# Loading keys and queries twice instead of copying the rounded half across partitions

## The chip, the core and the metric

The kernel runs on one core of a Trainium2 chip. Five engines take part: TensorE (PE in the profile; PEld is its weight load), VectorE (DVE), ScalarE (ACT), GpSimd (POOL) and SyncE (SP), which here issues every DMA. The metric is the device time of one execution in microseconds (us). Before the change the median of three runs is 737.69 us (737.01 to 740.85).

## The reference

Three layers follow one another on B = 4 sequences of S = 576 positions. The first is attention with H = 8 heads of D = 64 and a bias from a running sum:

```python
scores = scale * np.matmul(q, k.transpose(0, 1, 3, 2))
cum = np.cumsum(np.maximum(s, 0.0), axis=-1)
bias = -(cum[:, :, :, None] - cum[:, :, None, :])
scores = np.where(causal, -1e9, scores + np.minimum(bias, 0.0))
attn = softmax(scores)            # max, exp, sum + 1e-9
x = matmul(attn, v)               # then heads side by side: [B, S, 512]
```

The second layer is a gated feed-forward block (w_in 512 x 1024, GELU, normalisation, a 576 x 576 mixing matrix w_sg, w_out), and the third a block with squared ReLU and a sigmoid gate (w_k, w_v, w_r). All products are in fp32 precision: each operand is split into a rounded part (fp32r, "hi") and the rest ("lo"), and hi*hi, hi*lo and lo*hi are summed.

## The kernel before, in words

The scores of a head are two matmuls with 128 contraction rows each (L236 and L237). For the first, `qa` holds the rounded query in partitions 0 to 63 and the query's rest in 64 to 127, and `ka` holds the rounded key in both halves: one matmul gives hi*hi + lo*hi. For the second, `QB` holds the rounded query in 64 to 127 and `KB` the key's rest there, and partitions 0 to 3 of both carry ones and the running sum (the bias), split in hi and lo.

A head's operands come about so. `kq` is loaded by one DMA of 128 partitions: keys in 0 to 63, queries in 64 to 127 (L202). A cast rounds the query into `QB[64:128]` (L214: on DVE, for head 0 on ACT), another rounds the key into `ka[0:64]` (L215: on DVE for heads 1 to 7, else on ACT). Since an engine's lanes don't cross partitions, two DMAs inside SBUF copy the rounded query to `qa[0:64]` (L216) and the rounded key to `ka[64:128]` (L217). GpSimd computes the two rests (`split_lo`, L66 with tiles `KB` and `qa`). Two small DMAs bring the running sum into `QB` and `KB` (L207, L208), from the tile `crt` for the first sequence and from `cumd` in DRAM later.

`kq`, `qa` and `ka` have two buffers each; `QB` and `KB` have two fixed tiles, and a third borrowed set (names ending in `_f`) for the first sequence. Heads are worked on in pairs (`attn_pair`): score chunks of up to 512 columns go into two PSUM buffers `sc`; DVE adds the mask and takes the row minimum of the negated scores (L261), ACT takes the exponential (L269), PE transposes the result (L284, L287, L295), and the products with V follow (L317). In the first sequence a `prologue` converts the weights w_in and w_sg between the score steps: for w_in ACT L73, DVE L74, L75 and L77, ACT L80, POOL L66 (tiles `syt`, `wv`). From the second sequence on the attention of the next sequence is interleaved with the feed-forward matmuls (L346) of the one before. The third layer follows attention.

The order on each engine is not written out by hand: a scheduler sets it when the program is built, from its own timeline. Every engine, SP with its DMA issues too, executes its list in that order, and a row that waits holds back those behind it.

Of the kernel before, what the change touches and what calls it, by code (L numbers as in the profile page):

```python
# [8 lines left out]
F32 = mybir.dt.float32  # L9
# [5 lines left out]
B, H, S, D = 4, 8, 576, 64  # L15
DM, DFF = 512, 1024
FH = DFF // 2
P = 128
# [18 lines left out]
def fused_kernel(ctx, tc, kqT, vL, s, w_in, g_ln, w_sgT, b_sg, w_out, mu_k, mu_r, w_k, w_v, w_r, out):  # L37
    nc = tc.nc
# [22 lines left out]
    def f32(ap):  # L61
        return ap.bitcast(F32)


    def split_lo(eng, lo, x, hi):
        eng.tensor_tensor(out=lo, in0=x, in1=f32(hi), op=ALU.subtract)  # L66
# [24 lines left out]
    at = ap_stack.enter_context(tc.tile_pool(name="at", bufs=2))  # L91
# [15 lines left out]
    with tc.high_priority():  # L107
# [19 lines left out]
        out=mask[:, 512:], in_=mask[:, 512:], pattern=[[-1, P]], compare_op=ALU.is_ge,  # L127
# [65 lines left out]
    def attn_pair(b, hp):  # L193
# [3 lines left out]
        for hh in range(2):  # L197
            h = 2 * hp + hh
            hd = b * H + h

            kq = at.tile([P, S], F32, tag="kq", name=f"kq{hd}", bufs=2)
            nc.sync.dma_start(out=kq, in_=kqT[b, h])  # L202
            i = hd % (NSET + 1) if first else hd % NSET
            qb, kb = QB[i], KB[i]

            csrc = cr[hd:hd + 1] if b == 0 else cumd[hd]
            nc.sync.dma_start(out=f32(qb[1:4:2]), in_=f32(csrc))  # L207
            nc.sync.dma_start(out=f32(kb[0:3:2]), in_=f32(csrc))  # L208
            if i < NSET:
                qa = at.tile([P, S], F32R, tag="qa", name=f"qa{hd}")  # L210
                ka = at.tile([P, S], F32R, tag="ka", name=f"ka{hd}")
            else:
                qa, ka = qaf, kaf
            (nc.scalar.copy if hd == 0 else nc.vector.tensor_copy)(qb[64:128], kq[64:128])  # L214
            (nc.vector.tensor_copy if 0 < hd < H else nc.scalar.copy)(ka[0:64], kq[0:64])  # L215
            nc.sync.dma_start(out=f32(qa[0:64]), in_=f32(qb[64:128]))  # L216
            nc.sync.dma_start(out=f32(ka[64:128]), in_=f32(ka[0:64]))  # L217
            split_lo(nc.gpsimd, kb[64:128], kq[0:64], ka[0:64])
            split_lo(nc.gpsimd, qa[64:128], kq[64:128], qb[64:128])
            ops.append((qa, ka, qb, kb))  # L220
            if hh == 0:
                vf = at.tile([P, 2, NT, D], F32, tag="vf", name=f"vf{pr}", bufs=2)
                nc.sync.dma_start(out=vf, in_=vL[b][:, h:h + 2])
                x_t = ep.tile([P, S], F32, tag="xT", name=f"xT{pr}", bufs=8)
                xT[(b, hp)] = x_t
            yield 0
# [14 lines left out]
        for hh, i in steps:  # L241
# [8 lines left out]
            for ci, (c0, c1) in enumerate(chunks):  # L250
# [5 lines left out]
                else:  # L256
# [5 lines left out]
                    out=st[:, c0:c1], in0=sc[:, :n], in1=mk, op0=ALU.add, op1=ALU.min,  # L262
# [18 lines left out]
            tag = "acc" if first and i > 2 else "tp"  # L281
# [24 lines left out]
        for r in range(2):  # L306
# [3 lines left out]
            for kk in range(nk):  # L310
                o = max(0, kk * P - q0)
# [167 lines left out]


    pairs = [attn_pair(b, h) for b in range(B) for h in range(H // 2)]

    def a_stream():
# [68 lines left out]
    for b in range(B):  # L552
# [9 lines left out]
        kk = [kh, [kv[:, m] for m in range(KD)] + [ep.tile([P, S], F32R, tag="u", name=f"kl{b}_{m}", bufs=4) for m in range(KD, KF)]]  # L562
        for m in range(KF):
            f = slice(m * P, (m + 1) * P)
# [29 lines left out]
        for m in range(KD):  # L594
            if m + 1 < KD:
                gate(m + 1)
            f = slice(m * P, (m + 1) * P)
            o = ep.tile([P, S + 1], F32, tag="tmp", name=f"o{b}_{m}", bufs=3)[:, :S]
# [56 lines left out]
```

## Time and profile before

| | us |
|---|---|
| median of three runs | 737.69 |
| the profiled execution, its own time | 737.49 |
| its span (first to last instruction) | 735.4 |
| PE busy | 681.5 (93%) |
| DVE busy | 417.9 (57%) |
| ACT busy | 364.9 (50%) |
| POOL busy | 317.5 (43%) |
| mean granted TensorE clock | 0.981 |

A busy share is an average over stages with different limits, so it is read by stage: the first sequence's attention alone, then attention beside feed-forward, then the last layer. Idle time of an engine matters where the next engine in the chain waits for it.

### The profile page before, as it was taken

What the parts mean: (1) busy time and instruction counts of PE and PEld (TensorE: products, weight loads), DVE (VectorE), ACT (ScalarE), POOL (GpSimd) and SP (SyncE); (2) the same over time, 40 slices, a digit from 0 to 9 for tenths busy, and PEclk for the clock granted to TensorE, in tenths of its full rate; (3) what the DMA queues carried; (4) which work ended last, traced back from release to release, by engine and by line L of the source; (5) the groups of instructions that cost most, each with busy time, mean ns of one, the idle gap of its engine ahead of it and who ended that gap; (6) DMA issues with size and microseconds to landing.
All of it is one profiled execution on the core that took longest, in us unless ns stands there. A gap on an engine that the chain in (4) does not pass through costs nothing.

```text
span 735.4 us, 12753 instructions
## 1 busy us (share of the span) xinstructions
PE 681.5 (93%) x4720; PEld 610.6 (83%) x4720; DVE 417.9 (57%) x857; ACT 364.9 (50%) x839; POOL 317.5 (43%) x299
## 2 busy tenths in 40 slices
PE   2788899898999999999999969897999999999998
PEld 1555587777888878889877969896999999999997
DVE  4878675657662556573563799799444234403400
ACT  2767855555464565455562566367525234522400
POOL 6784663675352864264460665444511230320000
PEclk9999999999999999999999989998999999999999
DMA  6664433344534236424114762552220120000001
GB/s 181 196 168 150 154 96 129 117 118 144 148 103 123 78 81 176 141 66 134 52 38 131 248 217 62 179 160 74 81 66 1 49 80 3 1 33 33 2 17 48
DMA packets 33037, 74.95 MB, mean 102 GB/s; under 512 B 4368, under 2 KB 8464, under 8 KB 32976
## 3 DMA queue, kind: packets, MB, share of 16 engines
q1 hardware_dynamic: 32976, 74.15, 33.5%
q8 instruction: 37, 0.61, 0.4%
q14 instruction: 24, 0.20, 0.1%
HBM read 50.84 MB, written 13.79 MB: 88 GB/s over the span
## 4 chain that ended last, share of the span: by engine, by line
PE 63%; DVE 8%; DMA 3%; issue 3%; ACT 2%; POOL 1%; SPq 0%; DVEq 0%; ACTq 0%; POOLq 0%
PE vo L346 14%; PE k L346 10%; PE r L346 6%; PE pv L317 6%; PE sg L346 5%; PE o L346 5%; PE v L346 4%; PE u L346 3%; PE tp L287 3%; PE sc L236 3%; PE sc L237 2%; DVE lz L75 1%; DVE ly L77 1%; DMA lraw<-in_w_v_dram 1%; DVE lz L74 1%
## 5 line engine op out<-in xcount | busy, mean ns | idle before, releaser
L346 PE MATMUL k<-xvn,wk 128*128 128x288 f32 x768 | 104.4, 298 | 2.9 <-DVE y L450 2.9
L346 PEld LDWEIGHTS k<-xvn,wk 128*128 128x128 f32 x768 | 103.7, 190 | 3.1 <-DVE y L450 3.1
L269 ACT ACTIVATE st<-st,mx 128x128 f32<-128x128 f32 (+4 forms) x124 | 72.1, 583 | 52.1 <-DVE mx L261 50.5
L236 PE MATMUL sc<-ka,qa 128*128 128x512 f32 (+3 forms) x180 | 63.6, 359 | 26.7 <-DMA ka<-ka 13.9
L261 DVE CUSTOM_DVE_ANT_0 st<-sc,mask 128x512 f32<-128x512 f32 (+3 forms) x124 | 61.2, 503 | 33.5 <-PE sc L237 23.8
L346 PE MATMUL sg<-wsg,vn 128*128 128x288 f32 x448 | 70.1, 309 | 8.4 <-DVE vn L66 4.6
L346 PEld LDWEIGHTS sg<-wsg,vn 128*128 128x128 f32 x448 | 63.7, 196 | 11.7 <-DVE vn L66 4.8
L317 PE MATMUL pv<-pt,vf 128*64 128x320 f32 (+4 forms) x448 | 68.5, 375 | 0.5 <-ACT u L463 0.3
L236 PEld LDWEIGHTS sc<-ka,qa 128*128 128x128 f32 x180 | 33.4, 186 | 39.7 <-DVE mx L261 16.3
L66 POOL TENSOR_TENSOR KB<-kq,ka 64x576 fp32r<-64x576 f32 x30 | 43.4, 1448 | 44.8 <-ACT ka L215 31.5
L346 PE MATMUL vo<-kh,wvb 128*128 128x288 f32 x256 | 57.5, 298 | 4.5 <-ACT wvb L80 2.4
L606 DVE SCALAR_TENSOR_TENSOR o<-vo,sg 128x288 f32<-128x288 f32 x32 | 14.5, 456 | 80.8 <-PE vo L346 80.5
L66 POOL TENSOR_TENSOR xvn<-lt,xvn 128x576 fp32r<-128x576 f32 x16 | 27.6, 1738 | 74.8 <-ACT xvn L548 74.8
L317 PEld LDWEIGHTS pv<-pt,vf 128*64 128x64 f32 x448 | 37.0, 139 | 26.1 <-issue 7.7
L237 PE MATMUL sc<-KB,QB 128*128 128x512 f32 (+3 forms) x180 | 57.7, 335 | 0.4 <-DMA KB<-crt 0.4
L346 PE MATMUL vo<-kh,wva 128*128 128x288 f32 x256 | 56.9, 298 | 0.0
L346 PE MATMUL r<-xxs,wr 128*128 128x288 f32 x384 | 52.6, 294 | 0.0
L346 PEld LDWEIGHTS r<-xxs,wr 128*128 128x128 f32 x384 | 51.3, 188 | 0.0
L346 PE MATMUL v<-wv,xs 128*128 128x512 f32 x192 | 50.2, 401 | 0.7 <-ACT v L463 0.5
L575 ACT ACTIVATE lk<-k 128x288 f32<-128x288 f32 x64 | 26.0, 408 | 50.0 <-PE k L346 47.0
L66 POOL TENSOR_TENSOR qa<-kq,QB 64x576 fp32r<-64x576 f32 x30 | 43.7, 1456 | 13.2 <-DVE QB L214 8.2
L287 PE MATMUL tp<-ident,st 128*128 128x128 f32 x300 | 48.3, 277 | 0.7 <-DVE pt L298 0.4
(162 smaller groups left out, 1575.2 us busy)
## 6 DMA issues: line engine op xcount, KB each, us to landing
wc<-wscr SPq DMA_DIRECT2D x24, 512.0 KB
kq<-in_kqT_dram SPq DMA_DIRECT2D x32, 288.0 KB
vf<-in_vL_dram SPq DMA_DIRECT2D x16, 320.0 KB
ydram<-y SPq DMA_DIRECT2D x16, 288.5 KB
yt<-ydram SPq DMA_DIRECT2D x16, 288.5 KB
out_dram<-o SPq DMA_DIRECT2D x16, 288.0 KB
qa<-QB SPq DMA_DIRECT2D x30, 144.0 KB
ka<-ka SPq DMA_DIRECT2D x30, 144.0 KB
```

Source lines behind the costliest of these rows:

```text
L66: eng.tensor_tensor(out=lo, in0=x, in1=f32(hi), op=ALU.subtract)
L74: i1 = nc.vector.tensor_scalar(out=t, in0=lw, scalar1=2.0 ** -29, scalar2=7.0, op0=ALU.mult, op1=ALU.min)
L75: nc.vector.scalar_tensor_tensor(out=t, in0=hw, scalar=0x80000000, in1=t, op0=ALU.bitwise_and, op1=ALU.bitwise_or)
L236: nc.tensor.matmul(sc[:m, :c1 - c0], qa[:, q], ka[:, c0:c1], start=True, stop=False)
L237: nc.tensor.matmul(sc[:m, :c1 - c0], qb[:, q], kb[:, c0:c1], start=False, stop=True)
L261: nc.vector.tensor_tensor_reduce(out=st[:, c0:c1], in0=sc[:, :n], in1=mk, op0=ALU.add, op1=ALU.min, scale=-SCALE, scalar=mx[:, 0:1] if ci ...
L269: e = nc.scalar.activation(st[:, :w], st[:, :w], AF.Exp, bias=mx[:, last:last + 1], scale=-1.0, accum_out=sm[:, 4 * hh + i % 4:4 * hh + i ...
L287: nc.tensor.transpose(tp[:, c:c + P], st[:, j * P:(j + 1) * P], ident)
L317: nc.tensor.matmul(acc[64 * a:64 * a + 64, o:n], vf[:, a, kk], pt, start=(kk == 0), stop=(kk == nk - 1))
L346: nc.tensor.matmul(acc, a, w_, start=(i == 0), stop=(i == n - 1))
L575: nc.scalar.activation(t[:, c], acc[:, :HF], AF.Relu, scale=1.0 / WS)
L606: nc.vector.scalar_tensor_tensor(out=o[:, c], in0=acc[:, :HF], scalar=1.0 / WS, in1=sg[m][:, c], op0=ALU.mult, op1=ALU.mult)
```

## The change

The tile `kq` is replaced by `kk` and `qq`, which hold the key and the query in both halves of the partitions. Each is filled by two plain DMAs of 64 partitions from DRAM, so a head has four loads. The DMAs L216 and L217 go. The key's cast now covers 128 partitions in one instruction; the query's second half needs a cast of its own, on the same engine as the first (`cp`). The two subtractions on GpSimd keep their size and read the new tiles.

```diff
-            kq = at.tile([P, S], F32, tag="kq", name=f"kq{hd}", bufs=2)
-            nc.sync.dma_start(out=kq, in_=kqT[b, h])
+            kk = at.tile([P, S], F32, tag="kk", name=f"kk{hd}", bufs=2)
+            qq = at.tile([P, S], F32, tag="qq", name=f"qq{hd}", bufs=2)
+            for d, sl in ((qq, slice(64, 128)), (kk, slice(0, 64))):
+                for o in (64, 0) if d is qq else (0, 64):
+                    nc.sync.dma_start(out=d[o:o + 64], in_=kqT[b, h, sl])
...
-            (nc.scalar.copy if hd == 0 else nc.vector.tensor_copy)(qb[64:128], kq[64:128])
-            (nc.vector.tensor_copy if 0 < hd < H else nc.scalar.copy)(ka[0:64], kq[0:64])
-            nc.sync.dma_start(out=f32(qa[0:64]), in_=f32(qb[64:128]))
-            nc.sync.dma_start(out=f32(ka[64:128]), in_=f32(ka[0:64]))
-            split_lo(nc.gpsimd, kb[64:128], kq[0:64], ka[0:64])
-            split_lo(nc.gpsimd, qa[64:128], kq[64:128], qb[64:128])
+            cp = nc.scalar.copy if hd == 0 else nc.vector.tensor_copy
+            cp(qb[64:128], qq[64:128])
+            (nc.vector.tensor_copy if 0 < hd < H else nc.scalar.copy)(ka, kk)
+            split_lo(nc.gpsimd, kb[64:128], kk[64:128], ka[64:128])
+            split_lo(nc.gpsimd, qa[64:128], qq[64:128], qb[64:128])
+            cp(qa[0:64], qq[0:64])
```

The scheduler orders the whole program anew. In the changed kernel the lines from the cast on stand three or four lower (L214 is L218, L215 is L219, the new cast is L222, L207 and L208 are L210 and L211, L261 is L264).

On SP, at the program's start, the order before is as follows (the number after a tile's name is the head or the buffer; `sraw` is a piece of w_in, `bsg` a bias, `vf` the values):

```order
L202 DMA kq0_123<-in_kqT_dram 128x576
L223 DMA vf0_135<-in_vL_dram 128x640
L202 DMA kq1_138<-in_kqT_dram 128x576
L149 DMA sraw0_262<-in_w_in_dram 128x1024 x2
L54 DMA g_sb_64<-in_g_ln_dram 128x4
L216 DMA qa0_127<-QB0_81 64x576
L217 DMA ka0_128<-ka0_128 64x576
L55 DMA bsg_65<-in_b_sg_dram 128x576
L216 DMA qa1_142<-QB1_82 64x576
L207 DMA QB0_81<-crt_96 2x1x576
L208 DMA KB0_83<-crt_96 2x1x576
```

In the changed kernel the same place of SP's list reads:

```order
L205 DMA qq0_124<-in_kqT_dram 64x576 x2
L205 DMA kk0_123<-in_kqT_dram 64x576 x2
L226 DMA vf0_138<-in_vL_dram 128x640
L205 DMA qq1_142<-in_kqT_dram 64x576 x2
L205 DMA kk1_141<-in_kqT_dram 64x576
L210 DMA QB0_81<-crt_96 2x1x576
L211 DMA KB0_83<-crt_96 2x1x576
L205 DMA kk1_141<-in_kqT_dram 64x576
L210 DMA QB1_82<-crt_96 2x1x576
L211 DMA KB1_84<-crt_96 2x1x576
L149 DMA sraw0_268<-in_w_in_dram 128x1024 x2
L146 DMA cumd_62<-crt_96 32x1152
```

The 1 MB of w_in (`sraw`, twice 512 KB) stood ahead of the running sum's rows of the first two heads and now stands behind them, and ahead of the loads of head 2.

On DVE, at the end of the first pair of heads, the order before is (`st0_1_3` is the last score step of pair 0, `st_f1` the first steps of pair 1, `kq4` head 4, `rc` the softmax denominators):

```order
L261 ISA st0_1_3_249,mx0_1_3_250<-sc0_1_3_0_251,mask_80 128x512
L261 ISA mx0_1_3_250 128x1
L261 ISA st_f1_354,mx1_0_0_355<-sc1_0_0_0_356,mask_80 128x128
L261 ISA mx1_0_0_355 128x1
L261 ISA st_f1_354,mx1_0_1_361<-sc1_0_1_0_362,mask_80 128x256
L261 ISA mx1_0_1_361 128x1
L261 ISA st_f1_354,mx1_0_2_372<-sc1_0_2_0_373,mask_80 128x384
L261 ISA mx1_0_2_372 128x1
L214 CAST QB1_82<-kq4_535 64x576
L215 CAST ka4_540<-kq4_535 64x576
L74 TENSOR_SCALAR syt0_263<-sraw0_262 128x512
```

In the changed kernel DVE's list reads, from the same score step on:

```order
L264 ISA st0_1_3_255,mx0_1_3_256<-sc0_1_3_0_257,mask_80 128x512
L264 ISA mx0_1_3_256 128x1
L218 CAST QB0_81<-qq3_350 64x576
L74 TENSOR_SCALAR syt0_269<-sraw0_268 128x512
L304 TENSOR_SCALAR rc0_277<-sums0_89 128x9
L74 TENSOR_SCALAR syt0_269<-sraw0_268 128x512
L222 CAST qa3_357<-qq3_350 64x576
L75 SCALAR_TENSOR_TENSOR syt0_269<-sraw0_268,syt0_269 128x512
L305 RECIPROCAL rc0_277<-rc0_277 128x9
L75 SCALAR_TENSOR_TENSOR syt0_269<-sraw0_268,syt0_269 128x512
L219 CAST ka3_358<-kk3_349 128x576
L264 ISA st_f1_366,mx1_0_0_367<-sc1_0_0_0_368,mask_80 128x128
```

Three casts of head 3 and four rows of the w_in conversion now stand between the last score step of pair 0 and the first of pair 1.

## Rows read from the trace of the kernel before

**Rows 1.** The windows view: stretch in us, then each engine's busy us, clock, DMA share, GB/s.

```profile
0.00:14.00 14.00, 0.08 (x1) 0.11 (x1) 5.84 (x9) 3.19 (x4) 12.45 (x22) 1.00 0.70 199
14.00:90.00 76.00, 61.84 (x367) 43.75 (x367) 57.69 (x148) 54.46 (x149) 47.60 (x39) 0.96 0.57 163
90.00:403.00 313.00, 304.83 (x2069) 255.88 (x2068) 179.76 (x466) 170.21 (x428) 159.78 (x168) 0.99 0.38 111
403.00:735.00 332.00, 314.80 (x2288) 310.82 (x2288) 174.65 (x234) 137.06 (x258) 97.68 (x71) 0.97 0.23 75
```

**Rows 2.** Who PE waited for until 90 us: total us, times, longest.

```profile
PE sc L236 <- DMA ka<-ka: 13.9, 1, 13.9
PE sc L236 <- DVE mx L261: 11.1, 13, 2.3
```

**Rows 3.** The same view of PE from 90 to 400 us.

```profile
PE sc L236 <- DVE mx L261: 3.1, 4, 1.3
```

**Rows 4.** The timeline's first 20 us: start, duration, engine, line, instruction, idle before it.

```profile
4.13 0.67 ACT L214 CAST QB<-kq 64x576 fp32r<-64x576 f32 x1 [2.13 <-DMA kq<-in_kqT_dram]
...
4.82 0.67 ACT L215 CAST ka<-kq 64x576 fp32r<-64x576 f32 x1
...
5.40 0.67 ACT L122 CAST crt<-scr 32x576 fp32r<-32x576 f32 x1
...
6.11 1.39 POOL L66 TENSOR_TENSOR qa<-kq,QB 64x576 fp32r<-64x576 f32 x1
...
7.58 1.39 POOL L66 TENSOR_TENSOR KB<-kq,ka 64x576 fp32r<-64x576 f32 x1
...
8.64 0.64 DVE L214 CAST QB<-kq 64x576 fp32r<-64x576 f32 x1 [3.48 <-DMA kq<-in_kqT_dram]
...
9.69 0.78 DVE L66 TENSOR_TENSOR crt<-scr,crt 32x576 fp32r<-32x576 f32 x1
...
11.26 0.59 SPq L208 DMA_DIRECT2D KB<-crt  x1
...
15.11 0.76 PE L237 MATMUL sc<-KB,QB 128*128 128x128 f32 x2 [0.42 <-DMA KB<-crt]
...
15.59 0.29 DVE L261 CUSTOM_DVE_ANT_0 st_f<-sc,mask 128x128 f32<-128x128 f32 x1 [5.11 <-PE sc L237]
...
16.31 0.39 SPq L202 DMA_DIRECT2D kq<-in_kqT_dram  x1
...
19.32 0.46 DVE L214 CAST QB_f<-kq 64x576 fp32r<-64x576 f32 x1 [0.57 <-DMA kq<-in_kqT_dram]
```

**Rows 5.** The timeline: two casts on DVE, one beside a subtraction on POOL.

```profile
21.61 1.41 POOL L66 TENSOR_TENSOR KB_f<-kq,ka_f 64x576 fp32r<-64x576 f32 x1
...
21.82 1.52 DVE L214 CAST QB<-kq 64x576 fp32r<-64x576 f32 x1
...
28.21 0.46 DVE L214 CAST QB<-kq 64x576 fp32r<-64x576 f32 x1
```

**Rows 6.** DVE's groups by line, 14 to 77 us: count, busy us, mean ns, idle before.

```profile
L214 DVE CAST QB<-kq 64x576 fp32r<-64x576 f32 x6 | 5.2, 860 | 2.6 <-DMA kq<-in_kqT_dram 2.4
...
L215 DVE CAST ka_f<-kq 64x576 fp32r<-64x576 f32 x2 | 2.1, 1062 | 0.0
...
L215 DVE CAST ka<-kq 64x576 fp32r<-64x576 f32 x4 | 1.9, 477 | 0.1
...
L214 DVE CAST QB_f<-kq 64x576 fp32r<-64x576 f32 x2 | 0.9, 458 | 0.6 <-DMA kq<-in_kqT_dram 0.6
```

**Rows 7.** The same view of DVE, 90 to 403 us.

```profile
L214 DVE CAST QB<-kq 64x576 fp32r<-64x576 f32 x21 | 23.1, 1099 | 5.1 <-issue 3.4 <-PE sc L237 1.2
```

**Rows 8.** The windows view of two single us, columns as in the first group.

```profile
4.00:5.00 1.00, 0.00 (x0) 0.00 (x0) 1.00 (x1) 0.85 (x2) 0.95 (x2) 1.00 1.14 351
...
44.00:45.00 1.00, 1.00 (x8) 0.83 (x7) 0.55 (x2) 1.00 (x7) 1.00 (x1) 1.00 1.03 196
```

**Rows 9.** SP's timeline: the second of two loads of 64 partitions.

```profile
40.86 0.59 SPq L186 DMA_DIRECT2D wsr<-in_w_sgT_dram  x1
```

## The prediction, made before the changed kernel ran

> **What bounds the kernel now.** I read the windows view first, to see where PE, the busiest engine, is not busy [rows 1]. In the first 14 us it does nothing. From 14 to 90 us, the first sequence's attention, it is busy 61.84 of 76 us; from 90 to 403 us, attention beside feed-forward, 304.83 of 313. The change touches the operands of the scores, which are used up before 403 us, so what it can win there is PE's idle time: 14 us, 14.2 us and 8.2 us. The waits view says what ended it. Until 90 us one wait of 13.9 us ended with the DMA of `ka`, and 13 waits of 11.1 us in all with DVE's reduction L261, which frees a score buffer [rows 2]. From 90 us on, waits for that reduction are 3.1 us [rows 3]. So the DMA copies that the change removes hold PE once, at the start; afterwards the operands are there before PE wants them, and the engine behind PE's waits is DVE, busy 57.69 of the 76 us up to 90 [rows 1].
>
> The sum is made against the profiled execution's 737.49 us (span 735.4 and 2.1 around it); the median of the three runs is 0.2 above it.
>
> **The start: about 5 us won.** Before, the first score step needs three things: `ka` by DMA (PE's first matmul waits for it until 13.9), the subtractions on POOL, and the running sum's rows in `KB`, for which the second matmul waits until 15.11 [rows 2, 4]. Those rows come late because the split of `crt` stands on DVE behind the casts of head 1, which wait for their load until 8.64; it runs at 9.69, and its DMA into `KB` is issued at 11.26, behind 1 MB of `sraw` [rows 4]. In the changed order the split of `crt` stands ahead of the casts, and `sraw` behind the DMA. Step by step: the queries of head 0 are again 288 KB behind the same small load, so ACT's first cast starts near 4.13; three ACT instructions of 0.67 (two casts, then `crt`) end at 6.1; DVE's split takes 0.78, to 6.9 (before: 10.47); one issue of 0.59 later the `KB` rows go out at 7.5 [rows 4]. They are in place no later than the 15.11 - 11.26 = 3.85 us that it took before, at 11.4, and the step can't begin before POOL's two subtractions, from 6.11 and 1.39 each, at 8.9 [rows 4]. Between 8.9 and 11.4 I take 10: the 1 MB ahead is gone, but 752 KB (values, queries and half the keys of head 1) is there. That is 5 us earlier than 15.11, with 3.7 and 6.2 as ends.
>
> **The loads: about 1 us lost.** A head moves 576 KB either way (288 + 2 x 144 before, 4 x 144 now), so the bytes are equal, but all of them now go to 64 partitions at a time. The trace shows two rates with the DMA engines full: 351 GB/s while only loads of 128 partitions are under way, and 196 GB/s in a stretch in which two loads of 64 partitions, issued just before, are among them [rows 8, 9]. At the ends 0.8 to 1.5 us for 288 KB, so at most some 0.7 us more per head for the part that was one `kq` load. The Trainium skill (SBUF — State Buffer, Door 1: The DMA port swizzle) says that a transfer to partitions 0 to 63 reaches half the ports, 196 against 328 GB/s at 1 MiB, and that two transfers to the two halves run one after the other; the two rates above agree, and by the page's figures a head's four loads would take about 3 us, an estimate.
>
> What this does to the path: loads of heads 2 and 3 now stand behind `sraw`, `cumd` and `bsg`, 1,456 KB, which take 4.1 to 7.4 us from about 10. Head 2's queries then land at 15 to 19 (before: cast at 19.32, issued at 16.31 [rows 4]), and another 896 KB later, at 17.5 to 23.5, the queries of head 3, whose cast began at 21.82 before [rows 5]. In the changed list that cast stands on DVE ahead of all of pair 1's reductions, so DVE and then PE stand still if it is late. Pair 0's own steps, 5 us earlier, last until about 21 anyway, so the wait is 0 to 2.5; I take 1. The 64 copies that go win nothing more: no later wait of PE is on them.
>
> **The casts: about 4.4 us lost until 90 us.** A key cast over 128 partitions costs what it cost over 64: each lane still passes 576 elements. The new query cast is one instruction more per head: on ACT for head 0 (0.67, counted above), on DVE for 31 heads. One of them, head 1's, runs before the first reduction; eight (heads 2 to 9) fall between it and 90 us. The 14 casts on DVE between 14 and 77 us take 5.2 + 2.1 + 1.9 + 0.9 = 10.1 us, so 0.72 each [rows 6]; eight are 5.8 us. DVE is busy 57.69 / 76 = 76% of that stage, so I let three quarters lengthen it, 4.4 us, and the idle rest hide 1.4. The ends: 0 if they all fall into DVE's idle time, and 8 x 1.52 = 12.2 if each runs beside a subtraction on POOL, as one cast did that started 0.2 us after POOL and took 1.52, where another, with POOL idle, took 0.46 [rows 5]. I take the mean, since the new cast often stands right behind the one that POOL's next subtraction waits for, and is then through before POOL starts.
>
> **After 90 us: about 0.5 us lost.** 22 casts more at 1.10 [rows 7] are 24 us on DVE, 179.76 to 204 of 313 us [rows 1]. PE's matmuls of the feed-forward cover them. Without that cover each would delay a reduction, 24 us in all; but PE waits only 3.1 us for reductions there [rows 3], and scaled with DVE's load (204 / 180) that grows by 0.4. Both ends, 0 and 24, are kept in mind; the row is far nearer to 0. ACT and POOL get no instruction more. SP loses 64 issues that waited for casts and gets 96 loads, which wait only for a buffer two heads old; nothing queued behind them shows in PE's waits. The last layer has the same work and the same lines, and shifts as a whole.
>
> **Sum.** -5 + 1 + 4.4 + 0.5 = +0.9, so 738.4 against 737.49; with the 0.2 to the median 738.6. In words: the start is won, and DVE, which bounds the stage that follows, gives it back.
>
> **The rivals.**
> 1. The lead is kept (faster). The new casts find POOL idle, 0.46 each [rows 5], and DVE's 18.3 idle us before 90 [rows 1] take them in; loads come at 351 GB/s and nobody waits. Then -5 to -6.2 at the start, 0 to 8 x 0.46 x 0.76 = 2.8 back: 731.5 to 735.3, say 733. For it: 11.1 us of PE's waits were short waits spread over 13 places [rows 2], which a shifted order can close as well as open. Against it: DVE is the engine behind those waits.
> 2. POOL and DVE shut each other out (slower). The one mechanism: a cast issued while POOL subtracts ends only after it. If all eight take 1.52 and all of it is on the path, 12.2 - 5 + 1 + 0.5 = +8.7: 746.4. It decides for slower from about (3.7 + 5 - 1.5) / 8 = 0.9 us per cast, all on the path. For it: the mean after 90 us is 1.10 [rows 7]. Against it: 0.72 before [rows 6]. The Trainium skill has the rule (SBUF — State Buffer, Who interferes with whom): a copy that uses both of DVE's ports takes the port pair it shares with GpSimd for the whole instruction, and whichever issues second is blocked fully. The 1.52 against 0.46 agrees.
> 3. The first loads come late (no change to slower). At 196 GB/s throughout, head 3's queries land at 23.5 and the start is at 11.4: -3.7 + 2.5 + 4.4 + 0.5 = +3.7, 741.4. It needs the slow rate for the 128-partition loads too, which 351 GB/s speaks against [rows 8].
>
> **How the numbers follow.** A measurement of this kernel can tell about 0.5%, 3.7 us, from no change. The forecast (734.0 to 741.4, the lead given back) has 0.40, of which rival 3 is the upper edge with 0.08. Rival 1 has 0.28, rival 2 and the part of rival 3 beyond the edge 0.32, since each of three costs has a long upper end and only the start has a lower one. The forecast's own range is 735 to 741. The range for 8 in 10 reaches into both rivals, 731 to 746. So faster by over 0.5% 0.28, within it 0.40, slower 0.32.
>
> **What would show it.** Right at the start: the first reduction ends near 10.5 instead of 15.9, and the split of `crt` runs at about 6. DVE's busy time grows by 20 to 30 us, of it 4 to 8 before 90 us; the query casts average 0.7 to 1.1. DVE waits for `qq` loads about once before 30 us. The first matmul of the feed-forward's `v` starts within 3 us of where it did. It would be wrong if PE's idle time between its first matmul and 90 us stayed at 14 us (then rival 1), if the new casts averaged over 1.2 us with PE's waits for L261's successor growing by over 5 us (rival 2), or if the stretch after 90 us lost more than 3 us of PE's time.

## The result, and the profile after

The changed kernel took 747.87 us (median, 746.39 to 748.97), the kernel before 739.27 on the same chip (four executions each): ratio 1.0117, interval 1.0077 to 1.0156. It is slower, and above the predicted range, also above the 731 to 746 that was to hold 8 times in 10. The profiled execution has a span of 745.9 us against 735.4, so 10.5 us are to be found. The medians are only 8.6 apart: executions of one kernel differ by several us, and the profiled one of before (737.49, mean granted clock 0.981) is a short one. Later executions of before range from 735.74 to 743.25, and those with the 0.975 of the changed kernel's profile took 739.18 to 741.72. So two or three of the 10.5 us need not be the change's. I call *until pair 3* the time up to the start of the last `xT` of pair 3, the first sequence's last pair of heads (90.4 us before, 91.0 after), and *the rest* what follows it.

The start moved as far as predicted. These are rows of the timeline of the changed kernel (start, duration, engine, line, instruction, idle before it), which answer to [rows 4]:

```profile
5.99 0.75 DVE L66 TENSOR_TENSOR crt<-scr,crt 32x576 fp32r<-32x576 f32 x1 [0.82 <-ACT crt L122]
...
7.53 0.61 SPq L211 DMA_DIRECT2D KB<-crt  x1
...
8.71 1.40 POOL L66 TENSOR_TENSOR KB<-kk,ka 64x576 fp32r<-64x576 f32 x1
8.72 1.71 DVE L222 CAST qa<-qq 64x576 fp32r<-64x576 f32 x1 [0.34 <-DMA qq<-in_kqT_dram]
...
10.16 0.79 PE L240 MATMUL sc<-KB,QB 128*128 128x128 f32 x2 [1.31 <-POOL KB L66]
...
10.68 0.29 DVE L264 CUSTOM_DVE_ANT_0 st_f<-sc,mask 128x128 f32<-128x128 f32 x1 [0.25 <-PE sc L240]
```

The split of `crt` ran at 5.99, the `KB` rows went out at 7.53, and the first reduction began at 10.68 in place of 15.59: a lead of 4.9 us. What the first score step waited for last was not the running sum's DMA, though, but POOL's subtraction into `KB`, which ended at 8.71 + 1.40 = 10.11. The third and fourth rows already show the later trouble: the new cast L222 starts 0.01 us after a subtraction on POOL and takes 1.71 us, where one with POOL idle took 0.46 [rows 5].

The windows view of the changed kernel (stretch; busy us of PE, PEld, DVE, ACT, POOL; granted clock, DMA share, GB/s), first the stretches of [rows 1], then until pair 3 and the rest, and the rest once more in two parts, up to the start of attention's last `xT` (411 us) and behind it:

```profile
0.00:14.00 14.00, 4.09 (x11) 2.64 (x12) 9.46 (x17) 5.56 (x11) 12.52 (x22) 1.00 0.59 157
14.00:90.00 76.00, 59.75 (x343) 41.72 (x341) 61.66 (x145) 51.45 (x137) 52.51 (x38) 0.89 0.62 177
90.00:403.00 313.00, 301.18 (x2041) 253.78 (x2037) 194.92 (x491) 171.45 (x431) 160.67 (x168) 0.99 0.36 108
403.00:735.00 332.00, 314.69 (x2279) 308.81 (x2278) 173.94 (x233) 138.51 (x261) 99.90 (x71) 0.97 0.24 75
...
0.00:91.00 91.00, 64.85 (x362) 45.30 (x362) 71.69 (x162) 57.80 (x150) 65.18 (x61) 0.91 0.62 172
...
91.00:745.90 654.90, 622.23 (x4361) 568.77 (x4360) 369.67 (x727) 309.19 (x691) 260.42 (x238) 0.98 0.29 91
...
91.00:411.00 320.00, 308.18 (x2086) 258.80 (x2086) 195.93 (x494) 171.95 (x433) 160.51 (x167) 0.99 0.36 107
411.00:745.90 334.90, 314.05 (x2276) 309.97 (x2276) 173.74 (x233) 137.24 (x258) 99.90 (x71) 0.97 0.23 74
```

The last four of the kernel before (its last `xT` starts at 403.0):

```profile
0.00:90.40 90.40, 62.32 (x368) 44.22 (x369) 63.78 (x160) 57.65 (x153) 60.45 (x61) 0.96 0.59 168
...
90.40:735.40 645.00, 619.22 (x4353) 566.34 (x4352) 354.17 (x700) 307.27 (x686) 257.05 (x239) 0.98 0.30 93
...
90.40:403.00 312.60, 304.43 (x2066) 255.52 (x2066) 179.52 (x466) 170.21 (x428) 159.38 (x168) 0.99 0.38 112
403.00:735.40 332.40, 314.80 (x2288) 310.82 (x2288) 174.65 (x234) 137.06 (x258) 97.68 (x71) 0.97 0.23 75
```

So the loss is 0.6 us until pair 3, where the lead is gone, and 9.9 us in the rest, 7.4 of them before attention's last `xT` and 2.5 behind it. In the rest DVE is busy 15.5 us longer, PE idle (stretch less busy) 32.7 us in place of 25.8, and PE's matmul time 3.0 us longer, with 8 more matmuls on record; how far these 3.0 are only work moved over the mark is not shown. Whom PE waited for in the rest of the changed kernel (us in total, times, longest):

```profile
PE o L349 <- DVE gl L66: 5.3, 2, 3.4
PE sg L349 <- DVE vn L66: 5.0, 1, 5.0
PE sc L239 <- DVE mx L264: 3.9, 6, 1.3
PE sg L349 <- DVE ga L431: 3.0, 2, 2.3
...
PE k L349 <- DVE y L453: 2.1, 1, 2.1
PE o L349 <- DVE xT L334: 1.2, 2, 0.6
PE sg L349 <- DVE xT L334: 1.1, 1, 1.1
```

and of the kernel before:

```profile
PE sg L346 <- DVE vn L66: 4.6, 1, 4.6
PE sc L236 <- DVE mx L261: 3.1, 4, 1.3
PE k L346 <- DVE y L450: 2.9, 1, 2.9
...
PE sg L346 <- DVE ga L428: 2.2, 1, 2.2
...
PE o L346 <- DVE gl L66: 1.1, 1, 1.1
...
PE sg L346 <- DVE xT L331: 0.7, 1, 0.7
...
PE o L346 <- DVE xT L331: 0.4, 1, 0.4
```

These seven rows each sum to 21.6 us after and 15.0 before. The 6.6 us between them are nearly all of the 6.9 that PE lost. Few of the 6.6 are on a reduction (0.8). But only 2.8 of them (reductions, `ga`, `xT`) lie where the new casts run. The waits for `gl`, 4.2 us longer, lie behind attention: the last new cast starts at 377.1 us, and DVE's splits into `gl` run from 456.8 on. The waits for `vn` and `y` lie there too. So these rows name DVE, but don't show that its casts made the waits.

DVE's casts by line in the changed kernel from 91 to 411 us (count, busy us, mean ns, idle before), which answer to [rows 7]:

```profile
L218 DVE CAST QB<-qq 64x576 fp32r<-64x576 f32 x22 | 25.4, 1154 | 0.7
L222 DVE CAST qa<-qq 64x576 fp32r<-64x576 f32 x22 | 15.8, 717 | 18.9 <-PE sc L239 8.3 <-issue 7.5 <-PE sc L240 3.1
```

22 new casts are 15.8 us and not the 24 of the prediction. They stand ahead of L218 in DVE's list (L239 reads `qa`, and L240 behind it `QB`), and DVE is idle for 18.9 us before them: 8.3 until a matmul of L239, which reads `qa`, 3.1 until one of L240, and 7.5 in which the profile shows no wait. Before the change SP's DMA wrote this half of `qa`, so such a wait did not stand in DVE's list.

### The profile page after: what moved, and what is told of

Read it like the earlier page. It is cut to its first block, busy times and chain, and to the rows that moved or that the text cites. A ratio compares the mean times of both kernels' runs of the same rounds, so it can differ in the third digit from the quotient of the medians.

```text
span 745.9 us, 12774 instructions
## 1 busy us (share of the span) xinstructions
PE 687.1 (92%) x4720; PEld 614.1 (82%) x4720; DVE 441.4 (59%) x888; ACT 367.0 (49%) x840; POOL 325.6 (44%) x299
## 4 chain that ended last, share of the span: by engine, by line
PE 67%; DVE 17%; DMA 6%; issue 4%; ACT 3%; POOL 2%; SPq 1%; DVEq 0%; ACTq 0%; POOLq 0%
PE vo L349 14%; PE k L349 10%; PE pv L320 6%; PE r L349 6%; PE o L349 5%; PE sg L349 5%; PE v L349 5%; PE tp L290 3%; PE u L349 3%; PE sc L239 3%; PE sc L240 3%; DMA wr<-in_w_out_dram 2%; DMA lraw<-in_w_v_dram 1%; DVE lz L75 1%; DMA lraw<-in_w_k_dram 1%
## 5 line engine op out<-in xcount | busy, mean ns | idle before, releaser
L349 PE MATMUL k<-xvn,wk 128*128 128x288 f32 x768 | 102.9, 295 | 2.1 <-DVE y L453 2.1
L349 PEld LDWEIGHTS k<-xvn,wk 128*128 128x128 f32 x768 | 102.2, 188 | 2.3 <-DVE y L453 2.3
L239 PE MATMUL sc<-ka,qa 128*128 128x512 f32 (+4 forms) x180 | 64.7, 366 | 23.1 <-DVE mx L264 14.9
L264 DVE CUSTOM_DVE_ANT_0 st<-sc,mask 128x512 f32<-128x512 f32 (+3 forms) x124 | 61.4, 501 | 23.1 <-PE sc L240 17.2
L239 PEld LDWEIGHTS sc<-ka,qa 128*128 128x128 f32 (+1 forms) x180 | 33.7, 188 | 36.5 <-DVE mx L264 19.2
L66 POOL TENSOR_TENSOR KB<-kk,ka 64x576 fp32r<-64x576 f32 x30 | 45.4, 1513 | 40.8 <-ACT ka L219 34.0
L66 POOL TENSOR_TENSOR xvn<-lt,xvn 128x576 fp32r<-128x576 f32 x16 | 27.5, 1732 | 74.8 <-ACT xvn L551 74.8
L240 PE MATMUL sc<-KB,QB 128*128 128x512 f32 (+3 forms) x180 | 58.8, 338 | 1.3 <-POOL KB L66 1.3
L349 PEld LDWEIGHTS vo<-kh,wvb 128*128 128x128 f32 x256 | 44.2, 193 | 6.1 <-ACT wvb L80 3.4
```

The source lines that it names most:

```text
L239: nc.tensor.matmul(sc[:m, :c1 - c0], qa[:, q], ka[:, c0:c1], start=True, stop=False)
L240: nc.tensor.matmul(sc[:m, :c1 - c0], qb[:, q], kb[:, c0:c1], start=False, stop=True)
L264: nc.vector.tensor_tensor_reduce(out=st[:, c0:c1], in0=sc[:, :n], in1=mk, op0=ALU.add, op1=ALU.min, scale=-SCALE, scalar=mx[:, 0:1] if ci ...
L349: nc.tensor.matmul(acc, a, w_, start=(i == 0), stop=(i == n - 1))
```

## The experiments

The theories, as the expectations name them. A: the added cast on DVE costs; in A1 because a DVE copy and a POOL subtraction exclude each other (the lock), in A2 as one instruction more. B: the loads of 64 partitions are slow or late. C: the order of the lists. D: the new cast waits for PE to release `qa`, and DVE's list with it. E came last: DVE's busy time is covered up to a bend, and paid for above it. *The stage* in the expectations on E is the time from pair 3's last `xT` to the start of DVE's last split into `vn`, at 436.0 us before. A diff is against the changed kernel unless it says "before". At the end one table has all of them.

**Is it the cast, and is it DVE's?** `act_cast` puts it on ScalarE, `no_cast` takes it out (`qa`'s lower half stays zero in fixed tiles, so the product of the two rounded parts is left out), `before_cast` adds one that nothing reads to the kernel before.

```diff
 act_cast
-            cp(qa[0:64], qq[0:64])
+            nc.scalar.copy(qa[0:64], qq[0:64])
 no_cast
-            cp(qa[0:64], qq[0:64])
 before_cast, on before
+            (nc.scalar.copy if hd == 0 else nc.vector.tensor_copy)(spare[64:128], kq[64:128])
```

> The changed kernel with one edit: the new cast of the query's second half runs on ScalarE for every head instead of VectorE for heads 1 to 31. Theory A (VectorE's added work, partly spent waiting for GpSimd, is what cost the time): most of the 8.6 us goes, 738 to 742 us, VectorE busy back near 418 us, and the start keeps its first reduction near 10.7 us. Theory B (the loads of 64 partitions come late or slow): no change, 746 to 750 us. Theory C (the scheduler's new order of the same work): anything from 735 to 750, with the loss in other places than after.

> The changed kernel with all four loads per head, but without the query's second cast: the first 64 partitions of qa are fixed tiles set to zero once (so the product of the two rounded parts is left out of the scores). Theory A (the added instruction costs, whichever engine has it, in the first sequence, and VectorE's in the later ones too): as fast as key_twice, 731 to 736 us; first-sequence attention done (last xT) near 84 us instead of 91, and the stretch from there to the end of attention 313 to 316 us instead of 320. Theory B (the loads): stays at 744 to 749 us.

> The kernel before with one cast added per head: the query half of kq is rounded once more into a spare tile that nothing reads, on the same engine as the first cast; loads and copies stay. Theory A: slower by 6 to 12 us (745 to 751 against 739). Theory B: no change beyond 2 us. Theory C: a change of either sign, not tied to VectorE's busy time.

Measured 742.01, 736.63 and 749.34 us. The cast costs 11 us on DVE (747.9 - 736.6), 5.4 on ScalarE, and 9.8 in the old kernel, which has no new load and no wait for `qa`: A. (Its added cast does wait, 16.7 us in all, for the load of `kq`.) And since `no_cast` has all four loads and is a little faster than before (ratio 0.9966, 0.9945 to 0.9987), B is not the cause. It isn't the changed kernel without the cast in every respect: its first reduction begins at 14.75, since PE waits 4.7 us for the running sum's DMA, so it has little of the lead. A's range for it, 731 to 736, was just missed, and it reached pair 3 at 88.6 in place of the 84 that A named.

**The loads, with the copies kept.** `loads_copies` has four loads and the old casts and copies, 864 KB a head in place of 576.

```diff
-            cp(qb[64:128], qq[64:128])
-            (nc.vector.tensor_copy if 0 < hd < H else nc.scalar.copy)(ka, kk)
-            cp(qa[0:64], qq[0:64])
+            (nc.scalar.copy if hd == 0 else nc.vector.tensor_copy)(qb[64:128], qq[64:128])
+            (nc.vector.tensor_copy if 0 < hd < H else nc.scalar.copy)(ka[0:64], kk[0:64])
+            nc.sync.dma_start(out=f32(qa[0:64]), in_=f32(qb[64:128]))
+            nc.sync.dma_start(out=f32(ka[64:128]), in_=f32(ka[0:64]))
```

> The kernel before with the four loads of 64 partitions per head in place of the one of 128, while the casts and the two copies inside SBUF stay as before (half of what is loaded is not read). Per head 864 KB move instead of 576. Theory A: no change beyond 2 us, 737 to 741. Theory B: slower by at least what the change cost, 746 to 755. Theory C: either sign within 4 us.

746.84 us: 95.7 until pair 3 with a DMA share of 0.74 (0.59 before), and 4.1 more in the rest. That lies in B's range (746 to 755) and not in A's (737 to 741). But this kernel moves half as many bytes again per head, where the change moves as many as before: more bytes cost, mostly until pair 3, and equal bytes, in `no_cast`, did not.

**The key's half alone.** `key_twice` loads the key twice and casts it over 128 partitions, but loads the query once and copies it by DMA as before, so there is no added cast. `key_twice_h0` has head 0's query loaded twice as well.

```diff
 key_twice
-            for d, sl in ((qq, slice(64, 128)), (kk, slice(0, 64))):
-                for o in (64, 0) if d is qq else (0, 64):
-                    nc.sync.dma_start(out=d[o:o + 64], in_=kqT[b, h, sl])
+            nc.sync.dma_start(out=qq[64:128], in_=kqT[b, h, 64:128])
+            for o in (0, 64):
+                nc.sync.dma_start(out=kk[o:o + 64], in_=kqT[b, h, 0:64])
-            cp(qa[0:64], qq[0:64])
+            nc.sync.dma_start(out=f32(qa[0:64]), in_=f32(qb[64:128]))
 key_twice_h0, on key_twice
+            if hd == 0:
+                nc.sync.dma_start(out=qq[0:64], in_=kqT[b, h, 64:128])
-            nc.sync.dma_start(out=f32(qa[0:64]), in_=f32(qb[64:128]))
+            if hd == 0:
+                nc.scalar.copy(qa[0:64], qq[0:64])
+            else:
+                nc.sync.dma_start(out=f32(qa[0:64]), in_=f32(qb[64:128]))
```

> Half of the change: the key is loaded twice and cast over 128 partitions in one instruction, so its copy goes and no instruction is added; the query is loaded once and copied as before. Theory A: the start is won (first reduction near 11 us) and nothing given back: 732 to 737 us, faster than before. Theory B: slower than before by about half, 741 to 745. Theory C: between 735 and 745, whatever VectorE's busy time.

> key_twice with head 0's query loaded twice too and cast a second time on ScalarE, so that the first scores wait for no copy. Under theory A only the start moves: the first matmul from 8.9 to about 8 us, 732 to 734 us against 733.6. Under theory B nothing or slightly slower.

733.58 us, ratio 0.9931 (0.991 to 0.9952): faster than both kernels, and in A's range. Its first reduction begins at 12.50. With head 0's query 733.36, though that began at 11.24: the earlier start added nothing.

**Instruction or lock?** `before_reduce` adds to the kernel before a DVE row maximum over 384 columns, which is no copy. `swap_cast` only exchanges the two casts of before, as a null for C.

```diff
 before_reduce, on before
+            nc.vector.tensor_reduce(out=red[64:128], in_=kq[64:128, 0:384], op=ALU.max, axis=mybir.AxisListType.X)
 swap_cast, on before
-            (nc.scalar.copy if hd == 0 else nc.vector.tensor_copy)(qb[64:128], kq[64:128])
             (nc.vector.tensor_copy if 0 < hd < H else nc.scalar.copy)(ka[0:64], kq[0:64])
+            (nc.scalar.copy if hd == 0 else nc.vector.tensor_copy)(qb[64:128], kq[64:128])
```

> The kernel before with one VectorE instruction added per head that is as long as an unhindered cast (0.46 us) but has one input, writes one column and is no copy: a row maximum over 384 columns of kq. Theory A1 (what costs is that a VectorE copy and a GpSimd subtraction exclude each other): it costs less than half of the 9.8 us of before_cast, 739 to 743.5 us. Theory A2 (what costs is one more instruction and one more wait in VectorE's list): about the same as before_cast, 746 to 751 us.

> A null: the kernel before with the key's cast written ahead of the query's. The work is the same, the scheduler's order changes in places on VectorE, ScalarE and GpSimd and not on TensorE. Theory A: within 2 us of before. Theory C (order alone moves the time by several us): over 3 us to either side.

741.75 and 739.06 us. The row maximum averaged 549 ns where the spare copy averaged 845, and cost 2 us (ratio 1.002, 0.9998 to 1.0042) where that cost 9.8. That favoured A1, and C had no support from this one exchange. The table below corrects the first reading: in the rest the row maximum cost as much as the spare copy (650.6 and 650.9 us, 645.0 before), and the two differ until pair 3 (89.4 and 97.1).

**Casts that do not wait for POOL, and a third `qa`.** A maximum over one element is a copy in another form. `red_new` writes the new cast so, `red_all` all of DVE's casts, `key_twice_red` those of `key_twice`. `qa_three` gives `qa` three buffers and, for the room, the raw keys one.

```diff
 red_new (red_all, key_twice_red: the other casts too)
+    def reduce_cast(out, x):
+        out, x = (a.rearrange("p (n o) -> p n o", o=1) for a in (out, x))
+        nc.vector.tensor_reduce(out=out, in_=x, op=ALU.max, axis=mybir.AxisListType.X)
-            cp(qa[0:64], qq[0:64])
+            (nc.scalar.copy if hd == 0 else reduce_cast)(qa[0:64], qq[0:64])
 qa_three
-            kk = at.tile([P, S], F32, tag="kk", name=f"kk{hd}", bufs=2)
+            kk = at.tile([P, S], F32, tag="kk", name=f"kk{hd}", bufs=1)
-                qa = at.tile([P, S], F32R, tag="qa", name=f"qa{hd}")
+                qa = at.tile([P, S], F32R, tag="qa", name=f"qa{hd}", bufs=3)
```

> The changed kernel with its new query cast (heads 1 to 31) written as a maximum over one element, a VectorE instruction that reads one operand and, as the row maximum of 384 columns did (549 ns on average), should run beside a POOL subtraction at about 0.7 us. Theory A1 (a VectorE copy and a POOL subtraction exclude each other): the new instruction's mean stays near 0.7 us beside POOL, POOL's subtractions beside it stay near 1.1 us, and about 742 us, near the row-maximum kernel's cost of 2 us over the kernel without the new cast. Theory D (the new cast waits for PE to release qa, and VectorE's list waits with it): no change, 747 us, with idle time before the new instruction still 15 us or more. Theory A2 (one instruction more): 747 us or a little more, since it is longer than 0.46 us.

> The changed kernel with all three VectorE casts of a head written as a maximum over one element. A1: more than the single one gains, as the two old casts no longer wait for POOL or hold it: 738 us or less, casts near 0.7 us each, POOL's subtractions near 1.1 us. D: 747 us. A2: 750 us, since each cast alone is longer than a copy of 0.46 us.

> The changed kernel with three buffers for qa in place of two, and one in place of two for the raw keys to make the room (which can only delay a load). D: the idle time before the new cast falls from 18.9 us to a few, and 740 to 743 us. A1 or A2: 747 to 750 us.

> The kernel that loads the key twice and copies the query by DMA as before (733.6 us), with its two VectorE casts of a head written as a maximum over one element. A1: faster again, 728 to 731 us, since neither cast waits for POOL. A2: 734 to 736 us, since each is longer alone. D says nothing on it (no cast here waits for PE by a new order): 733.6 us.

Measured 750.96, 741.84, 757.96 and 741.6 us. No theory holds by these numbers: A1 missed all four, A2 all but `red_new`'s (747 or a little more), and D those of `red_new` (747), `red_all` (747) and `qa_three` (740 to 743) and the 733.6 that it left unchanged for `key_twice_red`. POOL's subtractions didn't come near the 1.1 us expected either: into `KB` they averaged 1527 ns in `red_new` and 1444 in `red_all`. `red_all`'s casts from 93.2 to 403.9 us:

```profile
L194 DVE TENSOR_REDUCE QB<-qq 64x576 fp32r<-64x576 f32 x21 | 15.7, 750 | 0.6
L194 DVE TENSOR_REDUCE qa<-qq 64x576 fp32r<-64x576 f32 x21 | 15.6, 741 | 17.4 <-issue 10.1 <-PE sc L244 7.1
```

`QB`'s cast fell from 1154 to 750 ns, as A1 has it, and `red_all` took 7.9 us less in the rest than the changed kernel although the idle time before `qa` stayed at 17.4 us. So D falls: that idle time doesn't have to be paid for. `qa_three` says the same from the other side:

```profile
L222 DVE CAST qa<-qq 64x576 fp32r<-64x576 f32 x29 | 27.4, 944 | 2.1 <-DMA qq<-in_kqT_dram 1.8
```

The idle time is gone (2.1 us in the whole run), the new cast takes 944 ns in place of 710, and the kernel is 10 us slower; the single buffer of raw keys may have a part in that. The two parts of the span had been mixed in these expectations: until pair 3 these kernels took 98.2, 93.2, 98.4 and 96.4 us, in the rest 653.2, 647.0, 658.4 and 646.6. Set against DVE's busy time, the rest had a rule, E, which three more runs were made to test.

**Only the rest.** `late_reduce` adds to the kernel before a row maximum over 512 columns from head 8 on; `act_late` puts the new cast on ScalarE from head 8 on; `key_twice_late` writes the query's cast in `key_twice` as a maximum over one element from head 8 on.

```diff
 late_reduce, on before
+            if hd >= H:
+                nc.vector.tensor_reduce(out=red[64:128], in_=kq[64:128, 0:512], op=ALU.max, axis=mybir.AxisListType.X)
 act_late
-            cp(qa[0:64], qq[0:64])
+            (nc.vector.tensor_copy if 0 < hd < H else nc.scalar.copy)(qa[0:64], qq[0:64])
 key_twice_late, on key_twice
-            (nc.scalar.copy if hd == 0 else nc.vector.tensor_copy)(qb[64:128], qq[64:128])
+            (nc.scalar.copy if hd == 0 else nc.vector.tensor_copy if first else reduce_cast)(qb[64:128], qq[64:128])
```

> The kernel before, with one row maximum over 512 columns (into a tile that nothing reads) per head for heads 8 to 31 on VectorE, some 0.65 us each, 16 us in all; no copy, no load and no buffer is changed. Theory E (VectorE's busy time above about 213 us is no longer covered in this stage): the first four pairs end at 90.4 us as before, VectorE is busy for about 222 us of the stage, the stage lasts 351 to 355 us in place of 345.7, and 745 to 748 us in all. Theories A1 and D (a lock with POOL, a wait for a buffer): neither is touched, so 739 to 741 us.

> The changed kernel with the new query cast on ScalarE for heads 8 to 31 (on VectorE for heads 1 to 7, as in the change). Theory E: VectorE is busy for about 205 us of the stage, which lasts 346 to 348 us; the first four pairs end at 91 us as in the changed kernel, and 740 to 742 us in all. If the order of the lists and not VectorE's time decides: no rule for the stage, anything up to 748 us.

> The kernel that loads the key twice and copies the query by DMA (733.6 us), with its query cast as a maximum over one element for heads 8 to 31 alone. Theory E: VectorE's busy time in the stage falls from 213 to about 207 us, below the bend, so the stage stays at 346 to 347 us, the first four pairs end at 84 us, and 732 to 734 us in all, no gain that can be measured. Theory A1 (each copy that waits for POOL costs): 729 us.

Measured 741.4, 741.13 and 731.58 us (the last: ratio 0.9898, 0.9873 to 0.9923, the fastest of all, but its interval overlaps that of `key_twice`; it lies just below E's range and nearer to it than to A1's 729). These are the windows of the rest in `late_reduce`, `act_late` and `key_twice_late`:

```profile
89.60:739.70 650.10, 620.51 (x4354) 565.51 (x4352) 363.88 (x720) 306.14 (x686) 257.90 (x239) 0.99 0.30 92
```

```profile
91.60:738.20 646.60, 619.93 (x4362) 567.91 (x4361) 354.64 (x703) 319.34 (x711) 258.10 (x238) 0.98 0.29 91
```

```profile
85.40:730.80 645.40, 620.43 (x4367) 567.27 (x4365) 353.20 (x705) 308.22 (x691) 255.58 (x238) 0.99 0.30 92
```

In `late_reduce` DVE's added 9.7 us, with no copy or load added, lengthened the rest by 5.1, 4.8 of them before attention's last `xT` (317.4 in place of 312.6); the stage took 350.3 us, where E said 351 to 355 and the others no change from 345.7. E's total (745 to 748) was missed, and the others' 739 to 741 nearly met, with a ratio to before of 1.0033 (1.0016 to 1.0051), so 1.2 to 3.8 us slower. One reason for the gap to 5.1 may be that before's profiled execution is a short one. E's total was too high because DVE's time in the rest did not grow by 15 us: 3.9 of the 16.4 us added show until pair 3 (67.73 against 63.78), and the kernel's own query casts took 2.6 us less (920 ns on average, before 1012). Nor does the row maximum add busy time alone:

```profile
L222 DVE TENSOR_REDUCE red<-kq 64x1 f32<-64x512 f32 x24 | 16.4, 682 | 13.9 <-DMA kq<-in_kqT_dram 13.5
```

It stands in DVE's list ahead of other rows and waits 13.5 us for its load, so this run alone doesn't tell busy time from a wait in the list. `red_all` speaks for busy time from the other side: it kept its wait, lost 11.2 us of DVE's time, and its rest was 7.9 us shorter. `act_late` came out as E said (740 to 742, and the stage at 347.4 in its 346 to 348); up to the last `xT` it took 312.7 us where the changed kernel took 320.0. The whole set, in the order of DVE's busy time in the rest (us, the first three columns of numbers from the one profiled execution):

| kernel | DVE busy, rest | rest | until pair 3 | median time |
|---|---|---|---|---|
| key_twice_red | 347.0 | 646.6 | 96.4 | 741.60 |
| act_cast | 350.9 | 647.5 | 92.7 | 742.01 |
| swap_cast | 353.0 | 645.3 | 90.3 | 739.06 |
| key_twice_late | 353.2 | 645.4 | 85.4 | 731.58 |
| no_cast | 353.9 | 646.0 | 88.6 | 736.63 |
| before | 354.2 | 645.0 | 90.4 | 739.27 |
| act_late | 354.6 | 646.6 | 91.6 | 741.13 |
| key_twice_h0 | 357.3 | 646.7 | 85.4 | 733.36 |
| red_all | 358.5 | 647.0 | 93.2 | 741.84 |
| key_twice | 358.8 | 647.3 | 84.0 | 733.58 |
| loads_copies | 360.6 | 649.1 | 95.7 | 746.84 |
| before_reduce | 361.0 | 650.6 | 89.4 | 741.75 |
| before_cast | 362.7 | 650.9 | 97.1 | 749.34 |
| late_reduce | 363.9 | 650.1 | 89.6 | 741.40 |
| red_new | 364.2 | 653.2 | 98.2 | 750.96 |
| after | 369.7 | 654.9 | 91.0 | 747.87 |
| qa_three | 376.0 | 658.4 | 98.4 | 757.96 |

Up to about 359 us of DVE the rest takes 645 to 647.5 us, in ten kernels. Above it the rest grows, by some 0.65 us for each us of DVE ((658.4 - 647.3) / (376.0 - 358.8) = 0.65). Both numbers are rough: each row is one execution, and the mark doesn't cut every kernel at the same work, with 355 to 374 matmuls on record ahead of it (`before` 368, `late_reduce` 368, the changed kernel 362, `act_late` 360, `key_twice` 355). The column until pair 3 follows no such rule.

## Why the prediction was wrong

- **The start, 5 us won: right**, 4.9, with the split of `crt` and its DMA at the times named (5.99 and 7.53). The last bit was luck: the 10 was picked between the end of POOL's subtractions, put at 8.9, and the landing of the DMA, put at 11.4 at the latest, with the DMA as what decides. It was the subtractions that decided; they ended at 10.11, since the first took 1.89 us and the second began at 8.71.
- **Until pair 3: right in sum, +0.6 after a predicted +0.4.** DVE was busy 7.9 us more there (63.78 to 71.69). PE's waits for reductions grew from 11.1 [rows 2] to 13.3 us, and its matmul time by 2.5 us for about as many matmuls at a lower granted clock (the mean of the stretch is 0.91, before 0.96). That these took the lead back is read from the profile; which did how much is not shown, nor that the change lowered the clock: the mean over the span is 0.975 after, and 0.968 to 0.986 in executions of before. That it was DVE's load is not shown either: `act_cast`, with 62.62 us of DVE here, took 81.5 us from its first reduction to pair 3, the changed kernel 80.3, before 74.8 and `no_cast` 73.9. So this part is longer with the cast on either engine. Late loads, the term of 1 us, had little part: DVE waited 1.5 us for `qq`, 1.2 of it ahead of the first reduction.
- **The rest: the step that failed is "PE's matmuls of the feed-forward cover them", +0.5 us; it was +9.9.** The casts were overestimated (24 us predicted, 15.8 between 91 and 411 us, 15.5 more DVE time in all the rest), and their price was put near nothing where it was about 0.6 us for each. The prediction's own sign of being wrong here, over 3 us of PE's time lost after 90 us, came true. I took the price from one wait, that for the reduction [rows 3], and scaled it with DVE's mean load. But DVE also makes the feed-forward's operands, and the matmuls covered only some 5 us more of DVE's time: the bend stood 4.6 us above where the kernel was (358.8 - 354.2). Three runs show together that DVE's time in the rest is what costs: `act_late`, in which only the new cast of heads 8 to 31 leaves DVE for ScalarE, took 8.3 us off the rest, 7.3 of them before attention's last `xT`, where 7.4 had been lost; `red_all`, with as many casts and nearly the same wait before `qa` but shorter casts, took 7.9 off (its median is 6.0 below; 374 matmuls stand ahead of its mark in place of 362); `late_reduce`, with other work on DVE in the kernel before, added 5.1. Which of PE's waits carries it is not shown: those for DVE's operands grew by only 2.8 us while casts ran.
- **Rival 2, POOL and DVE shut each other out**, had the right sign and a time 1.5 us too low, but the wrong place: it put the cost before 90 us, so that its number came near is luck. What the lock adds is DVE time: 1154 ns for a cast that takes 750 in a form that keeps clear of POOL, or 460 with POOL idle. The rule of the Trainium skill that the prediction names there (SBUF — State Buffer, Who interferes with whom) agrees with that. By the table it costs what any other DVE time costs. `red_new` lies some 2 to 3 us above its neighbours, but its profiled execution took 753.22 us, 2.3 more than its median.
- **Rival 3 and the loads' term**: `no_cast`, with all four loads, shows no loss: 73.9 us from the first reduction to pair 3 (before 74.8), and 646.0 in the rest (645.0).
- **The last layer, 0**: from attention's last `xT` (403.0 and 411 us) to the end it took 332.4 us before and 334.9 after, with waits for `gl` of 5.3 us in place of 1.1, in the last sequence's feed-forward. No new cast is left there, and DVE is busy no longer than before (173.7 and 174.7 us), so E doesn't explain these 2.5 us; in `act_late`, `red_all`, `red_new` and `qa_three` the wait for `gl` is 1.0 to 1.8, and this part still takes 333.9 to 336.3. What lengthens it is open.

Open: why the time until pair 3 ranges from 84.0 to 98.4 us. Each of these kernels has its own order of instructions there, and neither DVE's time nor the clock orders them, so C is not ruled out for this part. `key_twice` gains 6.4 us in it and loses 2.3 in the rest. Its first reduction comes 3.1 us earlier than before (12.50), its waits for reductions are 6.8 us in place of 11.1 [rows 2], and some work has moved behind the mark (355 matmuls ahead of it in place of 368); how these add up isn't shown.

## What to carry to other kernels

An engine that is busy 55% of a stretch can still lengthen it: look at all waits that it ends, on every operand it makes, and ask how far the stage is from the point where they grow. Measure that distance before you spend it, with a few added instructions that touch nothing else. `late_reduce` does this, except that its instruction waits for a load; one that reads a tile long in place would be cleaner. And compare medians too: a profile is one execution. A copy that DMA queues made beside the work is cheap as long as nobody waits for it; taken to an engine in the middle of its list, it costs that engine's time, and the half of this change that adds no instruction to an engine is the half that made this kernel faster.

## What the runs showed of the hardware

- A maximum over one element copies 64x576 values in 736 to 750 ns on average in each of the four runs that have it. POOL's subtractions make no difference: in `red_all` one at 101.48 us, with POOL idle, took 0.74 us, and one at 102.87, inside a subtraction that ran from 102.63 to 104.03, took 0.75. The plain copy takes 460 with POOL idle, and in the rest of the changed kernel 717 (`qa`) and 1154 (`QB`) on average.
- POOL's subtractions lose little to the copies: L66 into `KB` averaged 1513 ns in the changed kernel and 1444 in `red_all`. So nearly all of the delay fell on DVE's copies here.
